# A two-layer mixer block on one core: the program without a block and its closing barrier, and the last tile's stores issued by ScalarE

## The chip, the cores and the metric

The kernel runs on one core of a Trainium2 chip. The core has five engines with instruction streams of their own: TensorE (PE) for matmuls, VectorE (DVE), ScalarE (ACT) and GpSimd (POOL) for the rest, and SyncE (SP), which issues most of the transfers here. The metric is the time of one execution on the device, in microseconds; lower is better. The time given is the median of several executions. The span of the profile is something else: it runs from the first to the last record of the program in the trace, and is shorter than the time of the execution.

## The reference: what is computed

For 2048 tokens of width 512, in bfloat16: a layer norm, a matrix, GELU; then the four quarters of the features are shifted along the tokens by +1, -1, +2 and -2, a second matrix, and the residual. Then a layer norm and an MLP of width 1792, again with the residual.

```python
def reference(x, w1, w2, w3, w4):          # x: 1 x 2048 x 512; w3: 512 x 1792
    B, S, D = x.shape
    h = _gelu(_layernorm(x, axis=-1) @ w1)
    c = D // 4
    g0 = jnp.pad(h[:, :, 0*c:1*c], ((0, 0), (1, 0), (0, 0)))[:, :S, :]
    g1 = jnp.pad(h[:, :, 1*c:2*c], ((0, 0), (0, 1), (0, 0)))[:, 1:, :]
    g2 = jnp.pad(h[:, :, 2*c:3*c], ((0, 0), (2, 0), (0, 0)))[:, :S, :]
    g3 = jnp.pad(h[:, :, 3*c:   ], ((0, 0), (0, 2), (0, 0)))[:, 2:, :]
    hs = jnp.concatenate([g0, g1, g2, g3], axis=-1) @ w2
    x1 = x + hs
    h2 = _gelu(_layernorm(x1, axis=-1) @ w3) @ w4
    return x1 + h2
```

## The kernel before

The kernel has two parts. First it lists its operations, each with its engine, what it reads and writes, and an estimated duration, and a small scheduler in Python puts each engine's operations into an order before anything runs. Then `emit` writes them out as instructions with semaphores.

The tokens are 16 tiles of 128. The last stage, for each tile, is a chain of 14 matmuls into PSUM (`down`), the addition of the residual by VectorE into a buffer in SBUF, and a store to the output. The last tile is cut into three pieces, 256, 128 and 128 columns wide, so that less is left to do after the last matmul. All the stores are issued by SP.

```python
TAIL = (256, 128, 128)
...
        def mm_down(t):
            g = group_of[2, t]
            oi = t % NO                       # four output buffers
            last = t == NT - 1
            c0 = 0
            for hh, W in enumerate(TAIL if last else (D,)):
                b, v = next_bank()
                dst = o_ps[:, b, 0:W]
                cs = slice(c0, c0 + W)
                c0 += W

                def f(e, dst=dst, cs=cs):
                    for fc in range(FC):
                        ins = e.matmul(dst, h2T[:, fc, P * t : P * (t + 1)], w4_sb[:, fc, cs],
                                       start=(fc == 0), stop=(fc == FC - 1))            # line 511
                    return ins

                pg.add("pe", f"down{t}_{hh}", f, ...)
                pg.add("dve", f"res{t}_{hh}",                                           # line 519
                       (lambda d, c: (lambda e: e.tensor_tensor(o_sb[:, oi, c], d, x1_sb[:, t, c], ALU.add)))(dst, cs),
                       reads=[(("o", b), v), (("x1", t), 0)], writes=[(("osb", oi, hh), t)], dur=70 + W * 1.04)
                pg.add("sp", f"out_dma{t}_{hh}",                                        # line 522
                       (lambda c: (lambda e: e.dma_start(outt[:, t, c], o_sb[:, oi, c])))(cs),
                       reads=[(("osb", oi, hh), t)], dur=400 * W / D, queue="sp")
```

`emit` gives each transfer a semaphore of its own. It opens a block, in which every engine has a body; the instructions of each engine go into its body, and each waits for the semaphores of what it needs. At the end SP waits for every store. When the block is left, each engine drains and all five meet at a barrier.

```python
def emit(nc, es, prog):
    ...                                       # semaphores: one for each engine, one for each transfer
    with nc.Block() as block:                 # line 593
        bodies = {}
        ...
        block.gpsimd(keep("pool"))
        block.sync(keep("sp"))
        block.scalar(keep("act"))
        block.vector(keep("dve"))
        block.tensor(keep("pe"))
        ...
        for op in prog.seq:
            e = op.eng
            needs = {}
            ...                               # the semaphores and values that op has to wait for
            with nc.body(bodies[e]):
                for s, v in sorted(needs.items(), key=lambda sv: -sv[1]):
                    if k.get(s, 0) >= v:
                        continue              # known to be reached already
                    engs[e].wait_ge(sems[s], v)
                    ...
                ins = op.fn(engs[e])
                inc = 1 if op.queue is None else 16
                ins.then_inc(sems[op.stream], inc)
            ...
        with nc.body(bodies["sp"]):
            for op in prog.seq:
                if op.name.startswith("out_dma"):
                    nc.sync.wait_ge(sems[op.stream], 16)                                # line 655
```

Of the kernel before, what the change touches and what calls it, by code (L numbers as in the profile page):

```python
# [12 lines left out]
ENGINES = ["sp", "act", "pe", "dve", "pool"]  # L13
# [191 lines left out]
def bass_standalone__mixer_s_mlp__prompt_kernel(nc, x, w1, w2, w3, w4, out):  # L205
    B, S, D = x.shape
# [13 lines left out]
    with ExitStack() as es:  # L220
# [31 lines left out]
        pg = Program()  # L252
# [6 lines left out]
        def next_bank():  # L259
            nbank[0] += 1  # L260
            return (nbank[0] - 1) % NOB, nbank[0]
# [236 lines left out]
        def mm_down(t):  # L498
            g = group_of[2, t]
            oi = t % NO  # L500
# [11 lines that stand above are left out]
                                       start=(fc == 0), stop=(fc == FC - 1))  # L512
                    return ins

                pg.add("pe", f"down{t}_{hh}", f,
                       reads=[(("w4", c), 0) for c in range(FC)] + [(("h2", j, g), 0) for j in range(FC)],
                       writes=[(("o", b), v)], dur=FC * (W * 0.4167 + 2.5))
                pg.add("dve", f"res{t}_{hh}",
                       (lambda d, c: (lambda e: e.tensor_tensor(o_sb[:, oi, c], d, x1_sb[:, t, c], ALU.add)))(dst, cs),  # L519
                       reads=[(("o", b), v), (("x1", t), 0)], writes=[(("osb", oi, hh), t)], dur=70 + W * 1.04)  # L520
                pg.add("sp", f"out_dma{t}_{hh}",
                       (lambda c: (lambda e: e.dma_start(outt[:, t, c], o_sb[:, oi, c])))(cs),
                       reads=[(("osb", oi, hh), t)], dur=400 * W / D, queue="sp")


        consts()
# [15 lines left out]
        if SQRT:  # L542
            pg.add("act", "warm_sqrt", lambda e: e.activation(warm[:], eps_c[:], ACT_F.Sqrt),
                   reads=[(("eps",), 0)], writes=[(("warm",), 0)], dur=1400)
        pg.add("act", "warm_gelu", lambda e: e.activation(warm[:], eps_c[:], ACT_F.Gelu_apprx_tanh),
               reads=[(("eps",), 0)] + [(("sdv", q), 0) for q in SQRT], writes=[(("warm",), 1)], dur=1400)
        steps = []
        for step in SCRIPT.split():
            kind, n = step.split(":")
            a, _, b = n.partition("-")  # L550
            steps += [(kind, n) for n in (range(int(a), int(b or a) + 1) if kind != "warm" else [int(n)])]
        pe_tp = {n for kind, n in steps if kind in ("tp", "ty")}
        queue = []
# [11 lines left out]
        for kind, n in steps:  # L565
            if kind == "warm":
                warm_pe(n)
            elif kind in ("tp", "ty"):
                pe_transpose(n % NT, n, kind == "ty")
            elif kind == "mix":  # L570
                mm_mix(n)
            elif kind == "down":
                mm_down(n)
            else:
                for _ in mm_up(int(kind[2]), n):
                    pass
        pg.line(queue)
        pg.order()
        emit(nc, es, pg)

def emit(nc, es, prog):

    engs = {"sp": nc.sync, "act": nc.scalar, "pe": nc.tensor, "dve": nc.vector, "pool": nc.gpsimd}
    sems = {e: es.enter_context(nc.semaphore("sem_" + e)) for e in ENGINES}
    ndma = 0
    for op in prog.seq:
        if op.queue is not None:
            op.stream = ("dma", ndma)
            sems[op.stream] = es.enter_context(nc.semaphore(f"sem_dma{ndma}"))
            ndma += 1  # L590
        else:
            op.stream = op.eng
    with nc.Block() as block:
        bodies = {}

        def keep(name):
            def _body(e):
                bodies[name] = nc.cur_body

            return _body  # L600

        block.gpsimd(keep("pool"))
        block.sync(keep("sp"))
        block.scalar(keep("act"))
        block.vector(keep("dve"))
        block.tensor(keep("pe"))
        know = {e: {} for e in ENGINES}
        implied = {}
        count = {}
        last_write, readers = {}, {}  # L610
        for op in prog.seq:
            e = op.eng
            needs = {}

            def need(sv):
                if needs.get(sv[0], 0) < sv[1]:
                    needs[sv[0]] = sv[1]

            for res, ver in op.reads:
                lw = last_write[res]  # L620
                assert lw[2] == ver, (op.name, res, ver, lw)
                need(lw)
            for res, ver in op.writes:
                if res in last_write:
                    need(last_write[res])
                for sv in readers.get(res, ()):
                    need(sv)
            if e == "pe":
                needs.pop("pe", None)
            k = know[e]  # L630
            with nc.body(bodies[e]):
                for s, v in sorted(needs.items(), key=lambda sv: -sv[1]):
                    if k.get(s, 0) >= v:
                        continue
                    engs[e].wait_ge(sems[s], v)
                    for s2, v2 in implied[(s, v)].items():
                        if v2 > k.get(s2, 0):
                            k[s2] = v2
                    k[s] = max(k.get(s, 0), v)
                ins = op.fn(engs[e])  # L640
                inc = 1 if op.queue is None else 16
                ins.then_inc(sems[op.stream], inc)
            val = count[op.stream] = count.get(op.stream, 0) + inc
            snap = dict(k)
            snap[op.stream] = max(snap.get(op.stream, 0), val)
            implied[(op.stream, val)] = snap
            for res, ver in op.reads:
                readers.setdefault(res, []).append((op.stream, val))
            for res, ver in op.writes:
                last_write[res] = (op.stream, val, ver)  # L650
                readers[res] = []
        with nc.body(bodies["sp"]):
            for op in prog.seq:
                if op.name.startswith("out_dma"):
                    nc.sync.wait_ge(sems[op.stream], 16)


# [26 lines left out]
```

## Time and profile before

| | before |
|---|---|
| time, median of 3 runs | 139.0 us (138.16 to 139.03) |
| time of the profiled run | 137.98 us |
| span of its profile | 136.1 us |
| busy: TensorE, VectorE, ScalarE, GpSimd | 130.8, 59.0, 51.3, 19.4 us |
| stores: issues, KB each | 15 of 128 KB; for the last tile one of 64 KB, two of 32 KB |
| stores: issue to landing, median | 1.7 us for those of 128 KB, 1.5 us for the others |

In the profile, busy time is the time in which an engine works on data; waits, branches and the issue of transfers are not counted in it. A letter q after an engine (SPq, POOLq) means its sequencer, where those instructions are recorded. "L522" is line 522 of the kernel. A wait is written as "who waited <- on what: us in total, times, longest us". Durations in the list of one line's instructions are in ns (smallest, median, largest), followed by the start of the first and of the last one in us from the start of the span.

### The profile page before, as it was taken

What the parts mean: (1) busy time and instruction counts of PE and PEld (TensorE: products, weight loads), DVE (VectorE), ACT (ScalarE), POOL (GpSimd) and SP (SyncE); (2) the same over time, 40 slices, a digit from 0 to 9 for tenths busy, and PEclk for the clock granted to TensorE, in tenths of its full rate; (3) what the DMA queues carried; (4) which work ended last, traced back from release to release, by engine and by line L of the source; (5) the groups of instructions that cost most, each with busy time, mean ns of one, the idle gap of its engine ahead of it and who ended that gap; (6) DMA issues with size and microseconds to landing.
All of it is one profiled execution on the core that took longest, in us unless ns stands there. A gap on an engine that the chain in (4) does not pass through costs nothing.

```text
span 136.1 us, 2007 instructions
## 1 busy us (share of the span) xinstructions
PE 130.8 (96%) x787; PEld 73.4 (54%) x800; DVE 59.0 (43%) x170; ACT 51.3 (38%) x70; POOL 19.4 (14%) x43
## 2 busy tenths in 40 slices
PE   6799999999999999999999999999999999999993
PEld 2287788776668644444444444444444444444472
DVE  1888899998899640043610053210002222322231
ACT  4899657444566455530066630036660000000000
POOL 2441483333043310001010010000000000000000
PEclk9999999999999999999999999999999999999999
DMA  3999975574379551001210003110000111111121
GB/s 104 279 371 406 357 236 102 106 90 79 70 206 174 99 113 39 0 0 39 82 39 0 0 0 76 39 39 5 0 0 30 47 39 39 43 39 39 40 72 45
DMA packets 21401, 12.19 MB, mean 90 GB/s; under 512 B 13840, under 2 KB 20880, under 8 KB 21392
## 3 DMA queue, kind: packets, MB, share of 16 engines
q1 hardware_dynamic: 21248, 12.00, 33.4%
q8 instruction: 6, 0.10, 0.3%
q10 hardware_dynamic: 144, 0.07, 0.2%
q14 instruction: 3, 0.02, 0.1%
HBM read 6.82 MB, written 2.10 MB: 65 GB/s over the span
## 4 chain that ended last, share of the span: by engine, by line
PE 85%; DVE 5%; POOL 3%; DMA 2%; issue 1%; SPq 1%; ACT 0%
PE y_ps L442 40%; PE o_ps L511 35%; PE o_ps L482 9%; POOL rstd L366 3%; DMA x_sb<-in_x_dram 2%; DVE xn_buf L372 1%; DVE st L349 1%; PE y_ps L415 1%; DVE x_sb L493 1%; POOL xn_buf L383 1%; SPq L296 1%; DVE x_sb L489 1%; DVE mv L351 0%; DVE st6b L343 0%; DVE vpe L355 0%
## 5 line engine op out<-in xcount | busy, mean ns | idle before, releaser
L442 PE MATMUL y_ps<-xnT,w_sb 128*128 128x256 bf16 (+2 forms) x435 | 64.1, 305 | 0.3
L442 PEld LDWEIGHTS y_ps<-xnT,w_sb 128*128 128x128 bf16 x440 | 40.4, 98 | 23.7 <-issue 0.4
L511 PE MATMUL o_ps<-w_sb,h2T 128*128 128x512 bf16 (+2 forms) x250 | 48.8, 355 | 0.1
L457 ACT ACTIVATE h2T<-y_ps 128x1024 bf16<-128x1024 f32 (+1 forms) x29 | 28.6, 993 | 36.6 <-PE y_ps L442 36.6
L511 PEld LDWEIGHTS o_ps<-w_sb,h2T 128*128 128x128 bf16 x252 | 23.6, 98 | 25.2
L519 DVE TENSOR_TENSOR o_sb<-o_ps,x_sb 128x512 bf16<-128x512 f32 (+2 forms) x18 | 11.4, 632 | 44.3 <-PE o_ps L511 44.1
L366 POOL TENSOR_TENSOR rstd<-vpe,neghalf 128x1 f32<-128x1 f32 x31 | 16.9, 557 | 61.6 <-DVE vpe L355 49.6
L493 DVE TENSOR_TENSOR x_sb<-o_ps,x_sb 128x512 bf16<-128x512 f32 x14 | 9.6, 689 | 22.2 <-PE o_ps L482 22.2
L349 DVE BATCH_NORM_STATS2 st<-x_sb 128x6 f32<-128x512 bf16 x26 | 17.5, 684 | 2.2 <-DMA x_sb<-in_x_dram 2.0
L482 PE MATMUL o_ps<-w_sb,hT 128*128 128x512 bf16 x58 | 15.0, 379 | 0.3
L372 DVE TENSOR_SCALAR xn_buf<-x_sb,mv,rstd 128x512 bf16<-128x512 bf16 x25 | 10.2, 411 | 3.8 <-POOL rstd L366 2.8
L457 ACT ACTIVATE hT<-y_ps 128x1024 bf16<-128x1024 f32 (+1 forms) x10 | 8.4, 850 | 7.7 <-PE y_ps L442 7.6
L482 PEld LDWEIGHTS o_ps<-w_sb,hT 128*128 128x128 bf16 x64 | 6.1, 98 | 5.3
L535 PE MATMUL o_ps<-zeros 128*128 128x512 bf16 x12 | 4.3, 534 | 1.2 <-DVE zeros L269 1.2
L380 ACT ACTIVATE xn_buf<-x_sb,nmr,rstd 128x512 bf16<-128x512 bf16 x5 | 4.0, 809 | 2.6 <-DVE nmr L376 2.6
L351 DVE BATCH_NORM_AGGREGATE mv<-st 128x2 f32<-128x6 f32 x26 | 4.1, 173 | 0.2
L355 DVE TENSOR_SCALAR vpe<-mv 128x1 f32<-128x1 f32 x26 | 3.5, 148 | 0.3
L324 ACT ACTIVATE junk<-x_sb 128x512 bf16<-128x512 bf16 x5 | 3.1, 628 | 0.7 <-DVE x_sb L489 0.7
L535 PEld LDWEIGHTS o_ps<-zeros 128*128 128x128 bf16 x12 | 1.5, 131 | 3.5 <-issue 2.1
L415 PE MATMUL y_ps<-ident,xn_buf 128*128 128x128 bf16 x28 | 2.4, 220 | 1.0 <-DVE xn_buf L372 0.9
L415 PEld LDWEIGHTS y_ps<-ident,xn_buf 128*128 128x128 bf16 x28 | 1.8, 98 | 2.1 <-DVE xn_buf L372 1.6
L420 ACT ACTIVATE xnT<-y_ps 128x512 bf16<-128x512 bf16 (+1 forms) x5 | 2.6, 548 | 0.1
(33 smaller groups left out, 18.8 us busy)
## 6 DMA issues: line engine op xcount, KB each, us to landing
out_dram<-o_sb SPq DMA_DIRECT2D x15, 128.0 KB, 1.7
w_sb<-in_w_dram SPq DMA_DIRECT2D x1, 1792.0 KB, 9.8
w_sb<-in_w_dram SPq DMA_DIRECT2D x2, 896.0 KB, 9.4
x_sb<-in_x_dram SPq DMA_DIRECT2D x2, 512.0 KB, 11.2
x_sb<-in_x_dram SPq DMA_DIRECT2D x2, 256.0 KB, 4.4
w_sb<-in_w_dram SPq DMA_DIRECT2D x2, 256.0 KB, 3.7
w_sb<-in_w_dram SPq DMA_DIRECT2D x1, 512.0 KB, 5.5
x_sb<-in_x_dram SPq DMA_DIRECT2D x3, 128.0 KB, 2.4
```

The source lines that it names most:

```text
L349: pg.add("dve", f"bnst{q}", lambda e: e.bn_stats(st6[:, q, :], src), reads=rs, writes=[(("st6", q), 0)], dur=605)
L351: pg.add("dve", f"bnag{q}", lambda e: e.bn_aggr(mv[:, q, :], st6[:, q, :]), reads=[(("st6", q), 0)], writes=[(("mv", q), 0)], dur=75)
L366: lambda e: e.tensor_tensor(col(rstd), col(vpe), neghalf[:], ALU.pow),
L372: lambda e: e.tensor_scalar(dst, src, mv[:, q, 0:1], rstd[:, q : q + 1], ALU.subtract, ALU.mult),
L415: ins = e.transpose(chunk(c), xn_buf[:, slot(q), P * c : P * (c + 1)], ident[:])
L442: ins = e.matmul(y_ps[:, p, W * i : W * (i + 1)], wsb[:, dc, P * fc : P * (fc + 1)], src[:, dc, P * t0 : P * t0 + W], start=(dc == 0), sto ...
L457: (lambda d, s: (lambda e: e.activation(d, s, ACT_F.Gelu_apprx_tanh)))(dst, ysrc),
L482: ins = e.matmul(dst, hT[:, j, c0 : c0 + P], w2_sb[:, j, :], start=(j == 0), stop=(j == DC - 1))
L493: f = lambda e: e.tensor_tensor(x1_sb[:, t, :], dst, x_sb[:, t, :], ALU.add)
L511: ins = e.matmul(dst, h2T[:, fc, P * t : P * (t + 1)], w4_sb[:, fc, cs], start=(fc == 0), stop=(fc == FC - 1))
L519: (lambda d, c: (lambda e: e.tensor_tensor(o_sb[:, oi, c], d, x1_sb[:, t, c], ALU.add)))(dst, cs),
L535: ins = e.matmul(o_ps[:, b, :], zeros[:, 0:P], zeros[:], start=True, stop=True)
```

## The change

The block is taken away: the instructions of all engines are written straight into the program, and there are no bodies, no branches into them, and no drain and barrier behind them. SP's wait for all stores stays the last thing written. And for the last tile alone, the three stores are issued by ScalarE instead of SP, so that SP can go on to its final waits while the last tile is being finished. Everything else is the same. On each engine the remaining instructions stand in the same order as before.

```diff
@@ mm_down @@
-                pg.add("sp", f"out_dma{t}_{hh}",
+                pg.add("act" if last else "sp", f"out_dma{t}_{hh}",
                        (lambda c: (lambda e: e.dma_start(outt[:, t, c], o_sb[:, oi, c])))(cs),
-                       reads=[(("osb", oi, hh), t)], dur=400 * W / D, queue="sp")
+                       reads=[(("osb", oi, hh), t)], dur=400 * W / D, queue="act" if last else "sp")
@@ emit @@
-    with nc.Block() as block:
-        bodies = {}
-        ...
-        block.gpsimd(keep("pool"))
-        block.sync(keep("sp"))
-        block.scalar(keep("act"))
-        block.vector(keep("dve"))
-        block.tensor(keep("pe"))
     ...                                       # the loop over the operations moves one level out, and
-            with nc.body(bodies[e]):          # writes to the engine directly instead of into its body
     ...
-        with nc.body(bodies["sp"]):
-            for op in prog.seq:
-                if op.name.startswith("out_dma"):
-                    nc.sync.wait_ge(sems[op.stream], 16)
+    for op in prog.seq:
+        if op.name.startswith("out_dma"):
+            nc.sync.wait_ge(sems[op.stream], 16)
```

More of the change, by code (lines that the diff above doesn't have):

```diff
@@ L592, in emit @@
             op.stream = op.eng
-    with nc.Block() as block:
-        bodies = {}
[L596 to L600, printed above, removed]
-        block.gpsimd(keep("pool"))
-        block.sync(keep("sp"))
-        block.scalar(keep("act"))
-        block.vector(keep("dve"))
-        block.tensor(keep("pe"))
[L607 to L610, printed above, removed]
-        for op in prog.seq:
[L612 to L630, printed above, removed]
-            with nc.body(bodies[e]):
[L632 to L651, printed above, removed]
-        with nc.body(bodies["sp"]):
-            for op in prog.seq:
-                if op.name.startswith("out_dma"):
-                    nc.sync.wait_ge(sems[op.stream], 16)
@@ new lines, in emit, with need @@
+    know = {e: {} for e in ENGINES}
+    implied = {}
+    count = {}
+    last_write, readers = {}, {}
+    for op in prog.seq:
+        e = op.eng
+        needs = {}
+        def need(sv):
+            if needs.get(sv[0], 0) < sv[1]:
+                needs[sv[0]] = sv[1]
+        for res, ver in op.reads:
+            lw = last_write[res]
+            assert lw[2] == ver, (op.name, res, ver, lw)
+            need(lw)
+        for res, ver in op.writes:
+            if res in last_write:
+                need(last_write[res])
+            for sv in readers.get(res, ()):
+                need(sv)
+        if e == "pe":
+            needs.pop("pe", None)
+        k = know[e]
+        for s, v in sorted(needs.items(), key=lambda sv: -sv[1]):
+            if k.get(s, 0) >= v:
+                continue
+            engs[e].wait_ge(sems[s], v)
+            for s2, v2 in implied[(s, v)].items():
+                if v2 > k.get(s2, 0):
+                    k[s2] = v2
+            k[s] = max(k.get(s, 0), v)
+        ins = op.fn(engs[e])
+        inc = 1 if op.queue is None else 16
+        ins.then_inc(sems[op.stream], inc)
+        val = count[op.stream] = count.get(op.stream, 0) + inc
+        snap = dict(k)
+        snap[op.stream] = max(snap.get(op.stream, 0), val)
+        implied[(op.stream, val)] = snap
+        for res, ver in op.reads:
+            readers.setdefault(res, []).append((op.stream, val))
+        for res, ver in op.writes:
+            last_write[res] = (op.stream, val, ver)
+            readers[res] = []
@@ L659 @@
+    for op in prog.seq:
+        if op.name.startswith("out_dma"):
+            nc.sync.wait_ge(sems[op.stream], 16)
 _INS = ['x', 'w1', 'w2', 'w3', 'w4']
```

## The prediction

> **What bounds the kernel now.** I read the page from the top: the busy times, then the chain that ended last, and then, because the change touches only the two ends of the program, the last and the first microseconds in detail: the timeline, the waits of the DMA-issuing engine (SP) and the instructions of the lines concerned.
>
> ```profile
> PE 130.8 (96%) x787; PEld 73.4 (54%) x800; DVE 59.0 (43%) x170; ACT 51.3 (38%) x70; POOL 19.4 (14%) x43
> PEclk9999999999999999999999999999999999999999
> ...
> PE 85%; DVE 5%; POOL 3%; DMA 2%; issue 1%; SPq 1%; ACT 0%
> ```
>
> TensorE is busy for 130.8 of 136.1 us at the full granted clock, and 85% of the chain that ended last is TensorE. Nothing in the change takes a matmul away or moves one. What it can touch is what TensorE does not cover: the stretch from the last matmul to the end, and the stretch before the first useful matmul. So the whole question is the size of these two edges. The end, in the timeline from 132 us on (start, duration, engine, line, operation), and what SP did then:
>
> ```profile
> 132.31 0.42 DVE L519 TENSOR_TENSOR o_sb<-o_ps,x_sb 128x256 bf16<-128x256 f32 x1 [0.78 <-PE o_ps L511]
> 133.09 0.29 DVE L519 TENSOR_TENSOR o_sb<-o_ps,x_sb 128x128 bf16<-128x128 f32 x1 [0.36 <-PE o_ps L511]
> 133.87 0.29 DVE L519 TENSOR_TENSOR o_sb<-o_ps,x_sb 128x128 bf16<-128x128 f32 x1 [0.49 <-PE o_ps L511]
> ```
>
> ```profile
> SPq L522 <- DVE o_sb L519: 9.7, 6, 2.7
> SPq L655 <- DMA out_dram<-o_sb: 0.6, 1, 0.6
> SPq L593 <- PEq L593: 0.2, 1, 0.2
> ```
>
> Line 522 is the store, line 655 the final wait for the stores, line 593 the closing barrier of the block. These are the instructions of 655 in the stretch from 134.9 us, and then of 655 and 593 in the last 0.6 us:
>
> ```profile
> L655 SPq EVENT_SEMAPHORE  x3: 28/28/28, 134.9 to 135.0; - x3
> ```
>
> ```profile
> L655 SPq EVENT_SEMAPHORE  x1: 28/28/28, 135.7 to 135.7; - x1
> ```
>
> ```profile
> L593 POOLq EVENT_SEMAPHORE  x2: 17/17/17, 136.0 to 136.0; - x2
> L593 SPq COMPARE_BRANCH  x1: 33/33/33, 135.8 to 135.8; - x1
> L593 SPq DRAIN  x1: 13/13/13, 135.9 to 135.9; - x1
> L593 SPq EVENT_SEMAPHORE  x1: 17/17/17, 136.1 to 136.1; - x1
> ```
>
> The end is thus a short relay. The last addition ends at 133.87 + 0.29 = 134.16. SP issues the last store at 134.2 (its record is 332 ns long). It lands about 1.5 us after the issue. Between 134.6 and 135.0 SP walks through eight of its nine wait instructions (18 stores, two to an instruction); the ninth wakes at 135.7, when the last store has landed. Only then comes the closing part: a branch at 135.8, a drain at 135.9, GpSimd gathering the five engines at 136.0, and the release of all at 136.1, which is the end of the span.
>
> The stores that are to move are not held up by each other, as their issues show (the first line 133.4, the second 134.2; duration min/median/max):
>
> ```profile
> L522 SPq DMA_DIRECT2D out_dram<-o_sb x1: 333/333/333, 133.4 to 133.4; - x1
> ...
> DMA to landing us min/median/max: 1.5/1.5/1.5
> ```
>
> ```profile
> L522 SPq DMA_DIRECT2D out_dram<-o_sb x1: 332/332/332, 134.2 to 134.2; - x1
> ```
>
> SP is free again 0.33 us after 133.4, at about 133.7, which is 0.4 us before the last addition is done. The other store of this tile is issued at 132.8, so there too SP is done before it is needed.
>
> [...] Of ScalarE the trace has only one issue, of 64 KB at the start, 2.2 us to landing, a load and not a store. [...] The time of the profiled run (137.98 us) is 1.88 us over its span; no record shows what fills this.
>
> **The change part by part.**
>
> 1. The opening branch of each engine goes. The trace has no record of these five instructions. SP's barrier event is at 0.6 us and its first load is issued at 0.72 us, with 0.07 us of "issue" in the chain. At most this 0.07 us can go. The opening barrier, on the program's own first line, stays. Expected: 0.0 to 0.07 us, taken as 0.03.
>
> 2. The order of instructions is unchanged on every engine but for the branches and the three stores: the same loads, the same transposes, the same 787 recorded matmuls in the same order. So the 130 us in the middle should be equal, and SP and the DMA queue see the first fifteen stores as before: 0 us.
>
> 3. Three stores go from SP to ScalarE. ScalarE's last work is an activation at 100.56 us that takes 1.02 us; it has been waiting for over 31 us when the first addition of the last tile is ready at 132.31 + 0.42 = 132.73. Each store waits for its own addition alone, on either engine, and for nothing else. The three additions end at 132.73, 133.38 and 134.16, gaps of 0.65 and 0.78 us. An issue takes 0.33 us on SP; ScalarE's one issue at the start is 0.39 us against SP's 0.40 and 0.42 for its first loads. So ScalarE isn't a bottleneck either. Issue and landing of the last: again 134.2 + 1.5 = 135.7. Expected: 0 us, with 0.1 us either way for another sequencer's wake-up.
>
> 4. SP can now walk through its earlier waits while the tail is still being computed. These are eight instructions, 134.6 to 135.0, about 0.45 us. But SP then waits 0.6 us more for the last store in any case. That walk is wholly under the landing: 0 us.
>
> 5. The closing barrier goes. From the end of the ninth wait (135.7 + 0.03) to the end of the span (136.1) is 0.4 us: branch, drain, gather, release. All of it stands after the last landing with nothing beside it, so all of it should go from the span. Expected: 0.4 us.
>
> Sum: 0.03 + 0 + 0 + 0 + 0.4 = 0.43 us, 0.3% of 139.0. The span should be 136.1 - 0.43 = 135.7 us.
>
> To this I add a guess for the part outside the span. Engines that reach the program's end early (GpSimd after its drain at 81.3, ScalarE, TensorE, VectorE) may do their closing work beside the last store instead of after a common release. The whole of what the trace doesn't show is 1.88 us; I grant 0.1 us of it. This makes 139.0 - 0.43 - 0.1 = 138.5 us.
>
> **The rivals.**
>
> *The end barrier is only replaced.* If the end of a program is followed anyway by a barrier that the trace doesn't record, the 0.4 us may go from the span and come back outside it. [...] Against it: such a barrier would then stand there now as well, on top of the one removed. It would give 138.9 to 139.0 us, with a shorter span.
>
> *ScalarE is slower at storing than SP.* Its queue has been used once, at 0.71 us. If an idle queue takes longer to start or its landing takes longer, the last store lands later by that much. For it: 2.2 us for its one transfer, but that was a 64 KB load among other loads (SP's own of that size took 2.8). [...] With 0.3 us more the gain is nearly eaten: 138.8 to 139.0 us.
>
> *The early finish is worth much more.* If most of the 1.88 us outside the span is per-engine work that can now start when each engine is done, up to some 1.5 us could go, with the 0.43: about 137.1 us. For it: four engines are done by 134.2. Against it: SP still ends last, and its own closing work would have to follow the last landing as now.
>
> *The straight program is fetched better or worse.* The instruction queues moved six packets with 0.10 MB and three with 0.02 MB, at 0.3% and 0.1% of the DMA engines, and no wait in the list is put down to them. TensorE is busy 76.63 us in the 77.00 us from 47 to 124, so there are no stalls for a better fetch to take away: 0 us, or a few tenths worse if the new layout puts a fetch at a bad place.
>
> **Range and chances.** The three runs before are 138.16, 139.0 and 139.03: they differ by 0.87 us, twice the gain that I work out. If the next runs fall like the lowest of these, the result is 138.16 - 0.53 = 137.6; if ScalarE is slower and the barrier only moves, it is 139.0 with a little of scatter above. I take 137.6 to 139.1. Two per cent is 2.78 us. A gain of that size would need the full 1.88 us outside the span and the 0.43 and more. A loss of that size would need something in the 130 us of matmuls to change, and their order doesn't. Hence 3% for faster by over 2%, 96% for within 2%, 1% for slower.
>
> **What the profile after would show.** Step 5 is right if there are no drain and event records of the closing barrier, and the last record is SP's wait for the last store, at a span near 135.7. Step 3 is right if ScalarE issues at about 132.8, 133.4 and 134.2 with records of about 0.33 us and 1.5 us to landing; a longer landing means the second rival. Step 4 is right if most of SP's final waits are over before 134 us and only the last stands after the additions. Step 2 is right if TensorE is busy for 130.8 us again and ends at the same 133.85. The first and third rivals show in the difference between the run's time and its span: about 2.3 us instead of 1.88 for the first, well under 1.5 for the third. I would be wrong in kind if TensorE's busy time or the start of the first matmul moved by more than some tenths of a microsecond.

## The result and the profile after

| | before | changed |
|---|---|---|
| time, median | 138.93 us (138.09 to 139.3) | 137.3 us (136.42 to 137.51) |
| ratio | | 0.9885, 95% interval 0.9842 to 0.9928 |
| time of the profiled run | 137.98 us | 136.42 us |
| span of its profile | 136.1 us | 135.1 us |
| time outside the span | 1.88 us | 1.32 us |

The changed kernel is faster by 1.6 us, about 1.2%. The direction was predicted and the size was not: 137.3 us lies 0.3 us under the range of 137.6 to 139.1. Ratios and ranges of spans, here and below, are those of the runs in the faster state; times are medians over all runs.

The head of the page and its chain by engine, after:

```profile
span 135.1 us, 1995 instructions
...
PE 131.0 (97%) x787; PEld 73.5 (54%) x800; DVE 58.8 (44%) x170; ACT 51.3 (38%) x70; POOL 19.4 (14%) x43
...
PE 88%; DVE 5%; POOL 2%; DMA 2%; issue 1%; ACT 0%
```

TensorE has the same matmuls and is as busy as before (131.0 us against 130.8). The end, in the timeline from 125 us on, with ScalarE's sequencer (ACTq) now issuing the three stores:

```profile
131.68 0.42 DVE L519 TENSOR_TENSOR o_sb<-o_ps,x_sb 128x256 bf16<-128x256 f32 x1 [0.78 <-PE o_ps L511]
132.14 1.77 ACTq L522 DMA_DIRECT2D out_dram<-o_sb  x3
132.46 0.29 DVE L519 TENSOR_TENSOR o_sb<-o_ps,x_sb 128x128 bf16<-128x128 f32 x1 [0.36 <-PE o_ps L511]
133.25 0.29 DVE L519 TENSOR_TENSOR o_sb<-o_ps,x_sb 128x128 bf16<-128x128 f32 x1 [0.49 <-PE o_ps L511]
```

The same stores among the instructions of line 522, then among the transfers (the last number is the time from issue to landing in us), then the final wait (now line 639), then the sum of SP's waits in it:

```profile
L522 ACTq DMA_DIRECT2D out_dram<-o_sb x3: 338/338/348, 132.1 to 133.6; - x3
```

```profile
out_dram<-o_sb ACTq DMA_DIRECT2D x1, 64.0 KB, 1.5
out_dram<-o_sb ACTq DMA_DIRECT2D x2, 32.0 KB, 1.5
```

```profile
L639 SPq EVENT_SEMAPHORE  x9: 28/28/28, 131.3 to 135.1; - x9
```

```profile
SPq L639 <- DMA out_dram<-o_sb: 3.3, 4, 1.6
```

SP starts on its nine final waits at 131.3 us, before the last tile's additions, and the last of them at 135.1 is the last record of the program. There are no drains and no gather behind it. From the end of the last addition (133.25 + 0.29 = 133.54) to the end of the span there are 1.56 us, where there were 136.1 - 134.16 = 1.94 us before: 0.4 us less, as worked out.

But the whole difference between the two profiled runs is 137.98 - 136.42 = 1.56 us. Two more parts make it up. The last addition itself starts at 133.25 instead of 133.87, that is 0.62 us earlier, though no matmul, addition or transfer before it was changed. And 0.56 us have gone from outside the span. The experiments take these two apart.

### The profile page after: what moved, and what is told of

It reads as the page before. It is cut to its first block, busy times and chain, and to the rows that moved or that the text cites. A ratio compares the mean times of both kernels' runs of the same rounds, so it can differ in the third digit from the quotient of the medians.

```text
span 135.1 us, 1995 instructions
## 1 busy us (share of the span) xinstructions
PE 131.0 (97%) x787; PEld 73.5 (54%) x800; DVE 58.8 (44%) x170; ACT 51.3 (38%) x70; POOL 19.4 (14%) x43
## 4 chain that ended last, share of the span: by engine, by line
PE 88%; DVE 5%; POOL 2%; DMA 2%; issue 1%; ACT 0%
PE y_ps L442 42%; PE o_ps L511 36%; PE o_ps L482 10%; DMA x_sb<-in_x_dram 2%; POOL rstd L366 2%; DVE st L349 1%; DVE xn_buf L372 1%; PE y_ps L415 1%; POOL xn_buf L383 1%; DVE x_sb L489 1%; DVE st6b L343 0%; DVE vpe L355 0%; DVE mv L351 0%; PE o_ps L415 0%; DVE x_sb L493 0%
## 5 line engine op out<-in xcount | busy, mean ns | idle before, releaser
L535 PE MATMUL o_ps<-zeros 128*128 128x512 bf16 x12 | 4.8, 579 | 1.2 <-DVE zeros L269 1.2
```

The costliest lines, as they stand in the source:

```text
L535: ins = e.matmul(o_ps[:, b, :], zeros[:, 0:P], zeros[:], start=True, stop=True)
```

## The experiments

Theory: the end barrier costs more than its records, because it also holds back engines that could do their closing work early ("early finish"); the 0.62 us in front are the chance landing of a load ("scatter"). Rivals: the stores on ScalarE are what pays; or the block, with its bodies and branches, costs the time by where the code lies. "Outside the span" is the time of a run less the span of its records, the median over the runs of a kernel; the single runs of a kernel lie within 0.08 us of it. All ratios below are to the kernel before on the same chip.

**The stores alone, and the block alone.** In the first the block stays and only the store lines of the diff are applied. In the second the block goes and the store lines are undone:

```diff
-                pg.add("act" if last else "sp", f"out_dma{t}_{hh}",
+                pg.add("sp", f"out_dma{t}_{hh}",
...
-                       reads=[(("osb", oi, hh), t)], dur=400 * W / D, queue="act" if last else "sp")
+                       reads=[(("osb", oi, hh), t)], dur=400 * W / D, queue="sp")
```

> The block and its closing barrier stay; only the three last stores are issued by ScalarE. Edge theory (all that was won hangs on the program's end): nothing won, ratio 1.000, within 0.3 us of before, and about 1.9 us outside the span as before (137.98 - 136.1). Store theory (SP's free hands are what pays): ratio near 0.989, 137.4 us. Step 3 of the prediction says 0 us: issues of about 0.34 us and 1.5 us to landing.

> No block and no closing barrier, the stores stay on SP. Edge theory: the same as the changed kernel, ratio near 0.989 and 1.3 to 1.4 us outside the span. Store theory: ratio near 1.000 or at best 0.997 for the 0.4 us of the barrier's records.

Measured: the stores alone give 138.2 us against 138.23, ratio 0.9995 (0.9968 to 1.0022), and 1.84 us outside the span, the kernel before having 1.83. No block with SP's stores gives 137.9 us, ratio 0.9944 (0.9923 to 0.9966), and 1.34 us outside. The store theory falls: with the block in place, moving the stores is worth nothing that can be seen, and their issue and landing are those of SP. Everything hangs on the end of the program. In the second kernel SP walks through its nine waits only after its last issue, and this costs nothing, as the last store is still on its way:

```profile
SPq L522 <- DVE o_sb L519: 12.3, 7, 2.7
SPq L639 <- DMA out_dram<-o_sb: 0.6, 1, 0.6
```

The edge theory had this kernel near 0.989, like the first measurement; 0.9944 is 0.5% short of it, though the two intervals just overlap. So either the stores help when there is no block, or the first 0.9885 held something that is not in the kernel.

**The barrier back without the block, and all engines late without a barrier.** The first puts one barrier of all engines behind the last wait. The second has no barrier, but the four other engines wait for the landing of the last store too:

```diff
     for op in prog.seq:
         if op.name.startswith("out_dma"):
             nc.sync.wait_ge(sems[op.stream], 16)
+    nc.all_engine_barrier()                                   # the first
```

```diff
+    end = [op.stream for op in prog.seq if op.name.startswith("out_dma")][-1]
+    for e in ("pool", "act", "dve", "pe"):                    # the second
+        engs[e].wait_ge(sems[end], 16)
```

> The changed kernel with one barrier of all engines put behind the last wait: all five engines again end together, but there is no block. Early-finish theory (other engines' closing work runs beside the last store): the gain is given back, ratio near 1.000, about 1.9 us outside the span and 0.4 us of barrier in it. Block theory (the bodies and branches cost the time, by the place of the code or its fetch): only the 0.4 us come back, ratio near 0.992, and 1.3 to 1.4 us outside the span.

> The changed kernel, in which TensorE, VectorE, ScalarE and GpSimd too wait for the landing of the last store, with no barrier: all end at the same moment, with nothing for the barrier. Early-finish theory: the time outside the span goes back to about 1.9 us, and the whole is 0.5 us over the changed kernel (ratio near 0.992). Barrier theory (it is the drain and barrier records themselves, with what hangs on them outside the span): like the changed kernel, ratio 0.989, 1.3 to 1.4 us outside the span.

Measured: with the barrier back 138.26 us, ratio 0.9988 (0.9965 to 1.001), and 1.82 us outside. With all engines late 138.08 us, ratio 0.9972 (0.9951 to 0.9993), and 1.83 us outside. The second one's ends are these, at the same moment as SP's last wait:

```profile
L642 ACTq EVENT_SEMAPHORE  x1: 17/17/17, 136.0 to 136.0; - x1
L642 POOLq EVENT_SEMAPHORE  x1: 17/17/17, 136.0 to 136.0; - x1
L642 DVEq EVENT_SEMAPHORE  x1: 21/21/21, 136.0 to 136.0; - x1
L642 PEldq EVENT_SEMAPHORE  x1: 51/51/51, 136.0 to 136.0; - x1
```

There is no barrier, no drain and no block here, and still the half microsecond outside the span is back. So it isn't the barrier's instructions and isn't the place of the code; it is that the engines reach the end late (1.83 us outside the span when all five do, 1.34 when SP alone does). The block theory and the barrier theory fall for this part, and the early finish holds. (Its ratios were expected at 0.992, reckoned down from 0.9885; what is left of a gain, 0.9972, is 0.4 us of 138.2, the records of the barrier alone.) The barrier without a block has a cost in the span of its own: its last wait starts at 135.9, and then

```profile
L640 POOLq EVENT_SEMAPHORE  x2: 17/17/17, 136.0 to 136.1; - x2
...
L640 SPq DRAIN  x1: 7/7/7, 136.0 to 136.0; - x1
L640 SPq EVENT_SEMAPHORE  x1: 17/17/17, 136.1 to 136.1; - x1
```

up to a span of 136.2: 0.2 to 0.3 us, where the block's end with its branch took 0.4 us.

**The changed kernel again, and which engine must not be late.** The first is the changed kernel unaltered. Then GpSimd alone, TensorE alone and, in a later run, VectorE alone wait for the last store beside SP. In the last of this group ScalarE takes all the final waits and SP none.

```diff
+    end = [op.stream for op in prog.seq if op.name.startswith("out_dma")][-1]
+    nc.gpsimd.wait_ge(sems[end], 16)           # or nc.tensor, or nc.vector
```

```diff
-            nc.sync.wait_ge(sems[op.stream], 16)
+            nc.scalar.wait_ge(sems[op.stream], 16)            # the last of the group
```

> The changed kernel once more, beside the same runs of the kernel before as the next three. Early-finish theory plus barrier: time outside the span 1.34 us; of the whole gain 0.49 us outside the span and 0.4 us inside, so the ratio should be 1 - 0.9/138.2 = 0.9935, near the 0.9944 of no block with SP's stores. Store theory (ScalarE's stores add to it without the block): the first 0.9885 comes again.

> The changed kernel with GpSimd alone also waiting for the last store. If the 0.49 us outside the span are the closing work of each engine side by side, one late engine beside SP costs nothing: 1.34 us outside. If GpSimd's closing work is the long one, 1.83 us outside and 0.5 us more in all. If engines close one after another in a chain, something between.

> The changed kernel with TensorE alone also waiting for the last store. Same reading: 1.34 us outside the span if TensorE's closing work isn't the long one, 1.83 us if it is, between the two if the engines close in a chain.

> The changed kernel with VectorE alone also waiting for the last store. If the engines close side by side and the longest one counts: 1.34 us outside the span if VectorE's closing work is no longer than SP's, at most the 1.83 us of all together if it is.

> The changed kernel with the final waits for the stores on ScalarE, which issues the last three, and none on SP: SP ends after its last issue at about 131 us, ScalarE ends last. If the closing work is alike on all engines: 1.34 us outside the span and the same time. If ScalarE's is longer: up to 1.83 us; if SP's was still the longest part: under 1.3 us, and the fastest kernel of all.

| who ends last, with the landing of the last store | outside the span | time | ratio (95% interval) |
|---|---|---|---|
| SP alone (the changed kernel again) | 1.34 us | 137.92 us | 0.9951 (0.9926 to 0.9975) |
| SP and VectorE | 1.42 us | 137.41 us | 0.9922 (0.9898 to 0.9947) |
| ScalarE alone | 1.47 us | 137.71 us | 0.9949 (0.9928 to 0.997) |
| SP and TensorE | 1.58 us | 138.21 us | 0.9973 (0.9949 to 0.9997) |
| SP and GpSimd | 1.87 us | 138.36 us | 0.9992 (0.9967 to 1.0017) |
| all five (above) | 1.83 us | 138.08 us | 0.9972 (0.9951 to 0.9993) |

One more wait on GpSimd, a single record that costs the span nothing, takes back the whole half microsecond:

```profile
L641 POOLq EVENT_SEMAPHORE  x1: 17/17/17, 136.6 to 136.6; - x1
```

Call the time from an engine's last record to the end of the run its closing. In these runs the time outside the span is set by one engine, the one with the longest closing among those that end late; the closings don't add up. If they did, the extra times over SP's 1.34 us would make for all five: 0.08 (VectorE) + 0.24 (TensorE) + 0.53 (GpSimd) over 1.34 makes 2.19 us, and 1.83 us was measured, GpSimd's own number within 0.04. My expectation for TensorE had put a value between the two ends down to a chain; in this reading it is simply an engine of middle length. Two readings are left, both guesses of mine, as no record shows what a closing consists of: each is work of the engine's own, done side by side, or each is what is left of a relay that passes through the engines in a fixed order, with GpSimd early in it (1.87 us left) and SP late (1.34). In both the latest of the five decides, and these runs don't tell them apart. By the column outside the span SP is also a better engine to end on than ScalarE, which costs 0.13 us more; the ratios (0.9951 and 0.9949) are too coarse to show it. The times and ratios of the table scatter with what is shown next, so the column outside the span is the sharp one.

The changed kernel again gave a ratio of 0.9951 and not 0.9885, so the stores don't add to it without the block either. The two ratios of it touch at their edges (0.9926 and 0.9928). What remains is the scatter.

**The landing of one load.** These are pieces of the chain of waits (start, duration, what) of the kernel before:

```profile
1.66 2.82 DMA x_sb<-in_x_dram
...
4.50 0.43 DVE st6b L343
...
133.87 0.29 DVE o_sb L519
```

of the changed kernel in its first profile:

```profile
0.72 2.21 DMA x_sb<-in_x_dram
...
2.96 0.69 DVE st L349
3.65 0.65 DVE st6b L343 x2
...
133.25 0.29 DVE o_sb L519
```

and of the same changed kernel in its second one:

```profile
1.65 3.40 DMA x_sb<-in_x_dram
...
5.08 0.43 DVE st6b L343
...
134.86 0.29 DVE o_sb L519
```

The load and its reader in that first profile of the changed kernel, where they are not in the chain:

```profile
x_sb<-in_x_dram SPq DMA_DIRECT2D x1, 64.0 KB, 2.1
```

```profile
L343 DVE BATCH_NORM_STATS2 st6b<-x_sb x2: 407/408/409, 3.6 to 3.9; 128x6 f32<-128x256 bf16 x2
```

Line 343 takes the statistics of the two 64 KB halves of the first token tile; one half is loaded from ScalarE at 0.7 us, the other from SP at about 1.65 us, third in its queue. The second L343 waits for the latter. It started at 4.50 in the kernel before and at about 3.90 in the first profile of the changed one (the last start of that line), where the chain no longer runs through this load at all, and at 5.08 when the changed kernel was profiled again. The last addition follows: 133.87 - 4.50 = 129.37 us and 133.25 - 3.90 = 129.35 us after it. (In the second profile it is 129.78, so something else added 0.4.) The same instruction, issued at the same time, lands 2.8, 2.1 and 3.4 us after its issue in the three profiles, and TensorE carries the delay to the end. This was tested by issuing the load earlier, in the changed kernel and in the kernel before. All other instructions keep their order; SP's later loads are issued almost 0.5 us earlier too, as one issue in front of them is gone, and the edit doesn't separate the two:

```diff
         pg.order()
+        named = {op.name: op for op in pg.seq}
+        half = named["dma_x0_0"]
+        half.eng = half.queue = "act"
+        pg.seq.remove(half)
+        pg.seq.insert(pg.seq.index(named["dma_x0_1"]) + 1, half)
         emit(nc, es, pg)
```

> The changed kernel, with the second 64 KB half of the first token tile also loaded from ScalarE, at about 1.1 us instead of SP's 1.65 us; nothing else moves. Scatter theory (the rest of the first 1.6 us was the chance landing of this load): the second L343 starts at about 4.1 to 4.3 us instead of 4.5 to 5.1, the span falls by some 0.5 us and scatters less: about 137.3 us, ratio 0.990. If the landing scatters for another reason: as the changed kernel, 0.995.

> The kernel before, with the same earlier load of that half. Scatter theory: about 0.5 us under before, ratio 0.9965, and 1.83 us outside the span. With the landing out of the way, the changed kernel with the early load should be 0.88 us (0.49 outside the span and 0.39 in it) below this one, and not 1.6 us.

Measured: the kernel before with the early half 137.96 us, ratio 0.9962 (0.994 to 0.9984), 1.82 us outside; the changed kernel with it 137.57 us, ratio 0.9916 (0.9891 to 0.9941), 1.31 us outside. The instructions of line 343 in the latter:

```profile
L343 DVE BATCH_NORM_STATS2 st6b<-x_sb x2: 407/408/410, 3.8 to 4.1; 128x6 f32<-128x256 bf16 x2
```

The half isn't waited for any more. The early issue is worth 0.38% in the kernel before, clear of noise, and 0.35% in the changed kernel, where the intervals overlap; both are near what was expected. So the early loads do set the end in part, and are a lever of their own. The expected narrower scatter did not come: the spans of the kernel before still ran from 135.6 to 137.4 us with the early half, against 136.3 to 137.9 without. The chain of the changed kernel with the early half shows another transfer that ends a wait, one of the transposed copies (each turns a normalised token tile for the matrix that follows):

```profile
1.17 2.43 DMA x_sb<-in_x_dram
...
25.03 4.16 DMA xnT<-xn_buf
...
134.19 0.29 DVE o_sb L519
```

The last addition is at 134.19 in spite of the early start. Between the two kernels with the early half the ratios differ by 0.46%, that is 0.64 us of 138.6, with 0.88 expected; the two intervals leave nearly half a microsecond either way. This pair does not measure the gain sharply; it is consistent with it, and the 1.6 us of the first measurement didn't come again. The changed kernel with the early half has the lowest ratio of these experiments, 0.9916 beside the 0.9951 of the changed kernel measured again, though the intervals overlap.

**What else scatters.** The record holds eleven profiles in which SP issues this load. From the second L343 to the last addition it is 129.35 to 129.37 us in six of them, two with a closing barrier and four without, so the change doesn't touch the middle; in the other five it is 129.56 to 130.15 us. In the two longest (the stores alone, and GpSimd late) the chain runs through a transposed copy as well, without any early load. With GpSimd late:

```profile
4.66 0.43 DVE st6b L343
...
25.64 4.16 DMA xnT<-xn_buf
...
134.81 0.29 DVE o_sb L519
```

134.81 - 4.66 = 130.15 us, about 0.8 us over the six. This copy takes 4.12 to 4.16 us to landing in the three profiles whose chain it is in; the copies issued from 22.4 to 27.6 us take 2.5 us in the profile of the kernel before and 2.5 to 3.6 us in the first one of the changed kernel. So the load is not the only source of scatter.

The times themselves fall into two groups. Of the 67 runs of the kernel before beside the first four experiments, 41 took 137.9 to 138.42 us and all others 138.63 or more; of the 22 runs with no block and SP's stores, nine took 137.2 to 137.5 us and all others 137.77 or more. The medians of the two lower groups are 138.15 and 137.27 us. Their difference, 0.88 us, is the 0.49 us outside the span and the 0.4 us of the barrier over again. (The groups were seen afterwards, not foretold, and beside the later experiments they run into each other.) In the first measurement four of the six runs of the kernel before took 138.86 us or more, and none of the changed kernel more than 137.51: much of the first 1.6 us is which runs happened to be drawn. What makes the groups is not shown; the late copy would have about the right size.

## Why the prediction was wrong in size

The term that failed is the guess of 0.1 us outside the span, where 0.49 us were measured. The rest of the miss is the scatter of six runs against six. In order:

*Step 1, the opening branch (0.03 us).* Right as far as can be seen: the first load is issued at 0.72 us in both.

*Step 2, the middle (0 us).* The work is equal (the same matmuls, 131.0 us busy against 130.8), but the prediction's test for it, that TensorE ends at the same 133.85 us, failed: the last addition came 0.62 us earlier. In this pair of profiles it is the landing of one 64 KB load, and not the change: in the eight later profiles without the block and with SP issuing it, the load took 3.0 to 3.5 us, not 2.1. The sum had no term for scatter, and the range took it from three runs. In the medians scatter is the larger part of the miss: with the 0.38 us of the barrier's records (1.94 - 1.56) and 0.49 us outside the span the time would be 138.93 - 0.87 = 138.06 us, inside the range, and the remaining 0.76 us of the measured 1.63 have no cause in the kernel that any run showed; that part was luck. When the changed kernel was measured again the ratio was 0.9951, and 0.9944 with SP's stores; 0.87 us of 138.5 would be 0.9937, within both intervals.

*Step 3, the stores on ScalarE (0 us).* Right: records of 0.34 us, gaps and landing as on SP, and alone 0.9995. The second rival (ScalarE slower at storing) falls with it. Of a store issued by ScalarE the profile before has no record, so that its landing would be SP's 1.5 us was an assumption; the runs showed 1.5 us. Nor does any run show the 0.1 us granted for the wake-up: the last store is issued 0.03 us after its addition ends on either engine (134.19 against 134.16 on SP, 133.57 against 133.54 on ScalarE).

*Step 4, SP's walk through the waits (0 us).* Right: five of the nine are over before 132 us in the changed kernel, and with the walk at the end instead the last 0.6 us are waited all the same. (The prediction's 9.7 us of SP's waits in front of its stores are those from 125 us on, not from 132; nothing hangs on it.)

*Step 5, the closing barrier (0.4 us).* Right: 0.4 us from the span.

*The guess of 0.1 us outside the span.* This is the term of the sum that was mis-sized: 0.49 us were measured, and with it the forecast would have been 139.0 - 0.43 - 0.49 = 138.1 us. The third rival had been put aside with "SP still ends last, and its own closing work would have to follow the last landing as now". That is true of SP, whose closing takes 1.34 us, and was not enough: what counted before was GpSimd's, 1.87 us when it alone is late beside SP, which could not start until the barrier let it go, though GpSimd had been idle since its last work at 81 us. The first rival (the barrier is only replaced by another) falls too: the time outside the span went down, from 1.83 us to 1.34, and not up.

What stays open: what the engines do in the time outside the span, as no record shows it, and whether they do it side by side or in a relay; how much of the first measurement's surplus was this load and how much other chance, as only one of its runs has a profile; and why the same load and the same copy land so differently.

## What to carry to other kernels

The closing barrier of this kernel cost its records, 0.4 us of the span, and beside them it made every engine end late, which cost 0.49 us outside the span. In a kernel that ends like this one, let each engine run out when its work is done, and let only the engine with the shortest closing, SP here with 1.34 us, wait for the last store. This is read from the time of the run less its span, which the profile alone doesn't give. And before a gain of 1% is explained from one pair of profiles, look for the first place where the two traces part: here it was a load in the first five microseconds that the change had not touched.

## What was not expected of the hardware

The time outside the span depends on which engine ends last: 1.34 us when it is SP alone, 1.42 with VectorE, 1.58 with TensorE, 1.87 with GpSimd, and 1.47 when it is ScalarE in SP's place. A barrier of all engines took 0.2 to 0.3 us in the span without a block and 0.4 us at the block's end. One and the same 64 KB load, issued at the same moment behind two others, took 2.1 us to landing in one profile and 2.8 to 3.5 us in ten others.
